# Splitting the last 256 queries of an attention kernel by token tile, with two one-tile FFNs side by side at the end, and limiting VectorE's share of the exps by its backlog

## The chip, the cores and the metric

One core of one Trainium2 chip. The metric is the device time of one execution in microseconds (us), lower is better; medians of several executions are quoted, and the 95% interval of the ratio where a verdict rests on it. The verdict limits are 2%.

Most of what follows hangs on one property of this program's executions: they come in two kinds, about 5 us apart, that differ in the mean clock that was granted to TensorE (PE). Where it matters I compare executions with a mean clock of 0.992 or more with each other ("high clock"), and those of 0.989 or less with each other ("low clock").

## The reference, cut to what matters

```python
def reference(A_x, A_wqkv, A_wo, B_x, B_w_gate, B_w_up, B_w_down, c, w_mod):
    # x: 1 x 2048 x 512 bf16; 32 heads of 16; FFN width 1792
    mod = (_silu(c) @ w_mod).reshape(...)            # sa, ca, ga, sb, cb, gb
    h = _layernorm(x) * (1 + ca) + sa
    x = x + ga * attention(h, A_wqkv, A_wo)          # softmax over 2048 keys, 32 heads
    h = _layernorm(x) * (1 + cb) + sb
    return x + gb * (_gelu(h @ w_gate) * (h @ w_up) @ w_down)
```

The softmax needs 32 x 2048 x 2048 exps. In blocks of 128 partitions x 512 columns that is 2048 blocks; the kernel calls one block a unit.

## The kernel before

The kernel is generated by a recorder with a small scheduler in it. While Python builds the program, the scheduler keeps a rough clock for each engine and decides in which order score matmuls (queries times keys), exps, PV matmuls (exps times values), "side work" (projections, FFNs of finished queries) and VectorE tasks are recorded. Each engine then runs its list in that order.

- ScalarE (ACT) takes three units at a time with one exp of 1536 columns. When VectorE (DVE) has room, it takes one of the three with a five-instruction polynomial, and ACT's exp is 1024 columns.
- Queries go in groups of 512, 512, 512, 256, 256. While the scores of one group run, the output projection, layernorm and FFN of the group before it run as side work through a single bank (`mi`) of PSUM, the memory that PE writes its results to.
- The last group has nothing behind it to hide under: `tail` does its projection, layernorm and FFN after the last exp.

```python
GROUPS = ((0, 512), (512, 512), (1024, 512), (1536, 256), (1792, 256))
...
RSTD = 13                     # 1/sqrt by 4 set-up steps and three Newton rounds of 3 tiny VectorE steps
...
# GELU of one chunk of the FFN, as side work
self.task([lambda: self.tt("dve", w, g, g, ALU.mult),
           lambda: self.ts("dve", w, w, GELU_C, 1.0, ALU.mult, ALU.add),
           lambda: self.tt("dve", w, w, g, ALU.mult),
           ("act", lambda: self.act(w, w, ACT.Tanh, scale=TANH_C0)),
           lambda: self.ts("dve", w, w, 1.0, None, ALU.add),
           lambda: self.tt("dve", w, w, g, ALU.mult)], ("gelu", gi, ci))
...
# may VectorE take the exp of unit g (15 to 18 units ahead)?
if (pos >= nsplit + 24 and len(active) < NACT and self.free["dve"] < t + 700
        and len(mem) == CH and slack > -100 and self.credit < 1024):
    g = pos + CH * LEAD
    ...
    if g >= nseq - 4 * LEAD or any(k not in self.have for k in self.keys(seq[g])):
        g = None
...
def tail(self, gi):           # the last 256 queries: two token tiles, one after the other
    ...
    for i in range(n):
        self.wo_mm(wob[i], gi, i, 7)
        self.wo_fin(wob[i], tiles[i])
        self.ln_stat(tiles[i])
    for f in self.ln2_steps(tiles):
        f()
    # ... transposes, then gate/up/down matmuls of both tiles together, 256 columns wide ...
    for i in range(n):
        self.down_fin(down[i], tiles[i])
```

`credit` counts how many matmul columns the side work is behind its plan (at most 4096): with 1024 or more, VectorE gets no exp.

The softmax here doesn't subtract the row's maximum and nothing guards it: scores larger than these inputs give would overflow.

## Time and profile before

| | before |
|---|---|
| device time, median of the first timed runs | 944.0 us (943.5 to 944.4) |
| device time of the profiled execution | 938.98 us (span 937.2) |
| first exp starts / last exp ends | 19.64 / 898.85 us |
| end after the last exp | 38.35 us |
| units that VectorE took | 149 of 2048 |
| time that ACT waited between exps | 1.1 us |

The profiled execution is 5 us faster than the timed ones.

The profile's page of the kernel before, its first lines (busy time and share of the span; then the busy share in 40 equal slices, in tenths):

```profile
span 937.2 us, 16746 instructions
PE 804.0 (86%) x6954; PEld 253.4 (27%) x6954; DVE 753.1 (80%) x1494; ACT 895.7 (96%) x756; POOL 7.2 (1%) x13
...
DVE  7735999999987999989997999988896772489643
ACT  6999999999999999999999999999999999999941
```

ACT is full from the first slices to the last two. VectorE is full only in between. PE's 86% contains dummy matmuls that the scheduler puts in when nothing else is there, so it is not a limit either.

The table by stage of the kernel before (stretch in us; its length; busy us and instruction counts of PE, weight loads, DVE, ACT and POOL; PE's granted clock; DMA share; GB/s):

```profile
core 0: us, PE busy (x) PEld busy (x) DVE busy (x) ACT busy (x) POOL busy (x), PEclk, DMA share, GB/s
50.00:100.00 50.00, 44.93 (x406) 16.49 (x404) 26.91 (x48) 49.85 (x44) 0.00 (x0) 1.00 0.24 84
750.00:800.00 50.00, 46.17 (x530) 15.33 (x525) 25.68 (x48) 50.00 (x39) 0.00 (x0) 1.00 0.06 16
900.00:937.00 37.00, 25.64 (x166) 16.62 (x166) 16.66 (x38) 6.49 (x10) 0.00 (x0) 0.90 0.02 8
```

VectorE has 23 of 50 us free near the start and 24 of 50 in 750 to 800 us while ACT is full. The last row is the end, where ACT is idle and PE's clock drops to 0.90.

The timeline of the kernel before, at the end (start, length, engine, line, operation, out<-in, shapes, count, and in brackets the idle time before it with what ended it):

```profile
878.74 20.10 ACT L304 ACTIVATE E<-ps_sc 128x1536 bf16<-128x1536 f32 x15
...
900.56 1.76 DVE L328 RECIPROCAL rb<-ps_mi 128x256 f32<-128x256 f32 x1 [0.79 <-PE ps_mi L291]
...
903.79 0.69 DVE L308 TENSOR_TENSOR xw<-ps_sc,ga 128x512 bf16<-128x512 f32 x1 [1.02 <-PE ps_sc L291]
...
910.27 0.74 DVE L316 TENSOR_SCALAR hreg<-xs,mv,rstd 128x512 bf16<-128x512 bf16 x2
910.74 1.25 PE L295 MATMUL ps_sc<-ident,hreg 128*128 128x128 bf16 x8 [6.77 <-DVE hreg L316]
...
912.23 5.70 PE L291 MATMUL ps_sc<-wreg,mreg 128*128 128x256 bf16 x32 [0.23 <-ACT wreg L304]
912.64 1.28 ACT L304 ACT_TABLE_LOAD   x1
...
934.60 0.42 DVE L308 TENSOR_TENSOR xs<-xs,xw 128x512 bf16<-128x512 bf16 x1
```

The last exp ends at 878.74 + 20.10 = 898.84. The softmax denominators, projection (903.79) and layernorm (910.27) of two tiles keep VectorE busy and PE waiting 6.77 us; then come 20 us of FFN on PE and two residual adds.

### The profile page before, as it was taken

What the parts mean: (1) busy time and instruction counts of PE and PEld (TensorE: products, weight loads), DVE (VectorE), ACT (ScalarE), POOL (GpSimd) and SP (SyncE); (2) the same over time, 40 slices, a digit from 0 to 9 for tenths busy, and PEclk for the clock granted to TensorE, in tenths of its full rate; (3) what the DMA queues carried; (4) which work ended last, traced back from release to release, by engine and by line L of the source; (5) the groups of instructions that cost most, each with busy time, mean ns of one, the idle gap of its engine ahead of it and who ended that gap; (6) DMA issues with size and microseconds to landing.
All of it is one profiled execution on the core that took longest, in us unless ns stands there. A gap on an engine that the chain in (4) does not pass through costs nothing.

```text
span 937.2 us, 16746 instructions
## 1 busy us (share of the span) xinstructions
PE 804.0 (86%) x6954; PEld 253.4 (27%) x6954; DVE 753.1 (80%) x1494; ACT 895.7 (96%) x756; POOL 7.2 (1%) x13
## 2 busy tenths in 40 slices
PE   7899888888888888888888888888898899888868
PEld 2333222222222222222222222222222233233325
DVE  7735999999987999989997999988896772489643
ACT  6999999999999999999999999999999999999941
POOL 3000000000000000000000000000000000000000
PEclk9999999999999999999999999999999999999999
DMA  8002700000000000000000000000000000000000
GB/s 292 1 1 66 226 6 13 13 13 14 13 13 13 2 13 13 13 19 20 24 13 2 13 12 13 13 14 21 11 25 14 13 8 20 24 13 8 19 12 12
DMA packets 31269, 25.05 MB, mean 27 GB/s; under 512 B 16061, under 2 KB 25978, under 8 KB 31194
## 3 DMA queue, kind: packets, MB, share of 16 engines
q1 hardware_dynamic: 28810, 22.42, 8.1%
q10 hardware_dynamic: 2384, 1.57, 0.6%
q8 instruction: 54, 0.88, 0.4%
q14 instruction: 21, 0.17, 0.1%
HBM read 21.36 MB, written 2.61 MB: 26 GB/s over the span
## 4 chain that ended last, share of the span: by engine, by line
ACT 90%; PE 4%; DVE 4%; DMA 1%; issue 0%; SPq 0%; DVEq 0%; ACTq 0%
ACT E L304 88%; PE ps_sc L291 3%; ACT wreg L304 3%; PE ps_mi L291 1%; DVE du L321 0%; PE ps_pv L291 0%; DVE st L344 0%; DVE xw L308 0%; DMA xs<-in_A_x_dram 0%; DVE dreg L316 0%; DVE nwt L308 0%; SPq L354 0%; DVE dt L316 0%; DVE sc_bf L316 0%; DVE kmo L316 0%
## 5 line engine op out<-in xcount | busy, mean ns | idle before, releaser
L304 ACT ACTIVATE E<-ps_sc 128x1536 bf16<-128x1536 f32 (+2 forms) x699 | 867.9, 1525 | 13.8 <-PE ps_sc L291 13.7
L291 PE MATMUL ps_pv<-E,vaug 128*17 128x512 bf16 (+1 forms) x2326 | 180.6, 337 | 1.5 <-ACT E L304 1.3
L291 PE MATMUL ps_sc<-qT,kme 32*128 32x512 bf16 (+1 forms) x1280 | 152.0, 340 | 27.7 <-ACT E L304 22.8
L291 PE MATMUL ps_sc<-qT,kmo 32*128 32x512 bf16 (+1 forms) x1280 | 153.2, 340 | 25.9 <-ACT E L304 21.3
L316 DVE TENSOR_SCALAR dt<-ps_sc 128x512 int32<-128x512 f32 x149 | 102.8, 690 | 38.2 <-PE ps_sc L291 35.2
L291 PE MATMUL ps_sc<-xs,ident 128*128 128x512 bf16 x271 | 90.3, 386 | 46.1 <-ACT E L304 43.5
L291 PE MATMUL ps_mi<-wreg,mreg 128*128 128x512 bf16 (+1 forms) x448 | 119.8, 357 | 8.7 <-DVE hreg L308 4.4
L321 DVE SCALAR_TENSOR_TENSOR ED<-du,dt 128x512 int16<-128x512 f32 x149 | 101.5, 683 | 1.3
L321 DVE SCALAR_TENSOR_TENSOR du<-du,dt 128x512 f32<-128x512 f32 x149 | 100.6, 681 | 0.2
L321 DVE SCALAR_TENSOR_TENSOR du<-dt 128x512 f32<-128x512 uint16 x149 | 100.1, 682 | 0.1
L291 PEld LDWEIGHTS ps_sc<-qT,kme 32*128 32x128 bf16 x1280 | 39.0, 91 | 143.3 <-ACT E L304 107.6
L291 PEld LDWEIGHTS ps_sc<-qT,kmo 32*128 32x128 bf16 x1280 | 39.4, 91 | 139.2 <-ACT E L304 101.0
L291 PEld LDWEIGHTS ps_pv<-E,vaug 128*17 128x17 bf16 x2326 | 45.9, 87 | 99.2 <-issue 89.5
L291 PE MATMUL ps_mi<-dreg,hreg 128*128 128x512 bf16 x210 | 67.2, 385 | 1.6 <-DVE xw L308 1.0
L316 DVE TENSOR_SCALAR dt<-dt 128x512 f32<-128x512 int32 x149 | 61.5, 416 | 0.6
L291 PE MATMUL ps_pv<-ED,vaug 128*17 128x512 bf16 (+1 forms) x170 | 56.3, 356 | 0.0
L291 PEld LDWEIGHTS ps_mi<-wreg,mreg 128*128 128x128 bf16 x448 | 35.2, 97 | 68.9 <-issue 32.0
L308 DVE TENSOR_TENSOR wreg<-wreg 128x1024 bf16<-128x1024 bf16 (+1 forms) x84 | 51.9, 618 | 0.8
L325 DVE CAST wreg<-ps_mi 128x512 bf16<-128x512 f32 x49 | 33.7, 688 | 19.2 <-PE ps_mi L291 18.5
L291 PEld LDWEIGHTS ps_sc<-xs,ident 128*128 128x128 bf16 x271 | 19.6, 97 | 99.4 <-ACT E L304 97.1
L291 PE MATMUL ps_mi<-hreg,wreg 128*128 128x512 bf16 x120 | 39.8, 386 | 1.5 <-DVE vaug L325 0.7
L308 DVE TENSOR_TENSOR hreg<-ps_mi,wreg 128x512 bf16<-128x512 f32 x49 | 33.7, 688 | 8.7 <-PE ps_mi L291 8.0
(109 smaller groups left out, 514.7 us busy)
## 6 DMA issues: line engine op xcount, KB each, us to landing
rb<-scr_rec SPq DMA_DIRECT2D x96, 64.0 KB, 2.0
mreg<-in_w_mod_dram SPq DMA_DIRECT2D x1, 2048.0 KB, 13.1
out_dram<-xs SPq DMA_DIRECT2D x16, 128.0 KB, 1.7
rb<-scr_rec SPq DMA_DIRECT2D x60, 32.0 KB, 1.8
mreg<-in_B_w_gate_dram SPq DMA_DIRECT2D x1, 1792.0 KB, 7.2
mreg<-in_B_w_up_dram SPq DMA_DIRECT2D x1, 1792.0 KB, 12.0
dreg<-in_B_w_down_dram SPq DMA_DIRECT2D x1, 1792.0 KB, 19.9
wreg<-in_A_wqkv_dram SPq DMA_DIRECT2D x3, 384.0 KB, 10.5
```

Of the source, the lines that this page charges most:

```text
L291: return self.rec("pe", lambda e: e.matmul(out, lhsT, rhs, start=start, stop=stop, tile_position=tp), [lhsT, rhs], [out], cost=(n, int(rhs ...
L304: return self.rec("act", lambda e: e.activation(out, in_, func, scale=scale, **kw), rd, wr, cost=self.cost("act", out, [in_], "act"))
L308: return self.rec(eng, lambda e: e.tensor_tensor(out, a, b, op), [a, b], [out], cost=self.cost(eng, out, [a, b], "tt"))
L316: return self.rec(eng, lambda e: e.tensor_scalar(out, a, s1, s2, **kw), rd, [out], cost=self.cost(eng, out, [a], "ts"))
L321: return self.rec("dve", lambda e: e.scalar_tensor_tensor(out, a, s, b, op0=op0, op1=op1), rd, [out], cost=self.cost("dve", out, [a, b], " ...
L325: return self.rec(eng, lambda e: e.tensor_copy(out, in_), [in_], [out], cost=self.cost(eng, out, [in_], "ts"))
```

## The change

Its intent: the last 256 queries stay one 256-wide unit for head quads 0 to 5 (a quad is four heads), but quads 6 and 7 are scored first for token tile 14 alone, then for tile 15 alone. Tile 14 is thus finished 32 units (about 14 us) before the last exp; its projection and layernorm run under the remaining exps, and at the end its FFN runs next to tile 15's softmax, projection and layernorm. Around this, VectorE's load is changed: exps may start at unit 16 instead of 152, but only with fewer than 8 runnable steps waiting and fewer than three unconsumed exps; GELU loses one pass; the Newton iteration for 1/sqrt loses one round.

```diff
-GROUPS = ((0, 512), (512, 512), (1024, 512), (1536, 256), (1792, 256))
+SETS = ((0, 512), (512, 512), (1024, 512), (1536, 256), (1792, 128), (1920, 128))
+QS = 6
+BACK = 8
+DPOS = 16
...
-    RSTD = 13
+    RSTD = 10
...
-                               ("act", lambda: self.act(w, w, ACT.Tanh, scale=TANH_C0)),
-                               lambda: self.ts("dve", w, w, 1.0, None, ALU.add),
-                               lambda: self.tt("dve", w, w, g, ALU.mult)], ("gelu", gi, ci))
+                               ("act", lambda: self.act(w, w, ACT.Tanh, scale=TANH_C0))], ("gelu", gi, ci))
...
-                self.tt("dve", self.prodT[...], mi[...], w[...], ALU.mult)
+                self.stt(w[...], w[...], 1.0, mi[:, 0:W * k], ALU.add, ALU.mult)
+                if b0 + kpb >= m:
+                    self.tt("dve", self.prodT[...], w[...], g[...], ALU.mult)
...
+        due = (ends[1] + 30, ends[2] + 30, ends[3] + 30, n - 32, n)
...
+        units = [((k,), qd) + SETS[k] for k in range(4) for qd in range(8)]
+        units += [((4, 5), qd, SETS[4][0], 2 * P) for qd in range(QS)]
+        units += [((k,), qd) + SETS[k] for k in (4, 5) for qd in range(QS, 8)]
...
-                if (pos >= nsplit + 24 and len(active) < NACT and self.free["dve"] < t + 700
+                if (pos >= DPOS and len(active) < NACT and sum(v >= 4 * rp for v in vec) < 3
+                        and self.backlog() < BACK and self.free["dve"] < t + 700
                         and len(mem) == CH and slack > -100 and self.credit < 1024):
...
-    def tail(self, gi):
+    def tail(self, ka, kb):
+        self.act(self.tcol[:, 0:1], self.tcol[:, 0:1], ACT.Gelu_apprx_tanh)
+        gens = [self.tail_end(kb), self.tail_ffn(ka, self.pv[:, :], range(0, 4), 0)]
+        # ... at each step the generator whose next matmul is ready first goes on ...
```

`due` says by which unit each FFN of the side work has to be done; the third-last FFN (tiles 12 and 13) must now end 32 units before the end instead of 9.

## The prediction

> **What bounds the kernel now.** ScalarE's exp. The page gives ACT 895.7 of 937.2 us busy (96%), and the chain of waits is ACT 90%. In the table by stage ACT is full (50.0 of 50) from 20 us to 898.9 us; then 38.3 us follow with ACT nearly idle. By shape, ACT runs 515 exps of 1536 columns and 177 of 1024, issued 1.34 and 0.92 us apart (timeline), so one 512-column unit costs ACT 0.43 us. VectorE takes 149 of the 2048 units, five instructions, about 3.2 us each. PE is filled up with 309 dummy matmuls (ps<-xs,ident); it does not bound. So only two things count: fewer units on ACT, and a shorter end.
>
> **The end (main gain).** In the timeline, after the last exp: 11.4 us of copy, reciprocal, output projection, layernorm (two tiles one after the other, 13 rstd steps 0.2 us apart) before the first transpose at 910.7; PE waits 6.8 us there and its clock falls (0.90 in this stretch); table load 1.28 us; FFN of two tiles to 932.4; two serial residual steps and a store to 937.2. The change finishes tile 14's attention 32 units (about 14 us) earlier, so its projection and layernorm run under the last exps and its FFN fills the time in which tile 15 goes through reciprocal, projection and layernorm. Matmuls of 128 columns cost no more per column: 16 took 1.07 us (57 ns each), 256-column ones 109 ns. So each one-tile FFN is about 112x57 ns + 14x213 ns = 9.4 us of PE. Estimate: tile 15's chain 9-10 us (half widths, 10 steps), then 9.4 us FFN, then 3.5-5 us: about 25 us instead of 38.3. Gain 13, less about 1 us for denser PE work and VectorE work near the end.
>
> **VectorE.** (a) Exps may start at unit 16 instead of 152. VectorE is busy 26.9 of 50 us in 50-100 us and never takes an exp before 88 us; I expect about 7 more there, 3 us of ACT. (b) GELU loses one 0.42 us pass per 1024-column chunk net (a 0.42 and a 0.68 us pass go, a 0.68 us one comes; the multiply from PSUM stays 0.69 us[...]). [...] About 9 us of VectorE, 2-3 exps, 1 us. (c) Three rstd steps fewer: 0.6 us on the chain before the first exp; elsewhere small. (d) The backlog limits delay exps but do not lower VectorE's capacity; in 100-700 us it is 93% busy anyway. In 700-850 us only 7 exps run, though VectorE has 50 us free; I think side-work credit holds them back, and the change leaves that as it is. I expect 155-165 exps in all.
>
> **Sum.** 13 - 1 + 3 + 1 + 0.6 = about 16 us: 928 us, range 921 to 937. Faster by over 2% means below 925: 0.33; within 2%: 0.63; slower: 0.04.
>
> **What would show it.** From last exp to end 23-28 us, with ps_sc<-wreg,mreg matmuls starting within about 2 us of the last exp, and PE clock near 1.0 there. ED count 155-165 with several before 88 us. ACT still 100% busy from 19 us to about 900.
>
> **What would make it wrong.** Tile 14's layernorm not ready at the last exp (its side work queues behind the third-last FFN, which must now end 23 units earlier): the end stays above 30 us. ACT waiting for PE in the last 28 us, where scores and PV come in twice as many 128-column matmuls. The limit of three unconsumed VectorE exps cutting them in 150-700 us: each lost costs 0.43 us. Or the better VectorE order letting many more exps in at 700-850 us: then 920.

(13 - 1 + 3 + 1 + 0.6 is 16.6, put as about 16, and 944 - 16 is 928. The 1 us taken off for denser work near the end was an allowance of mine with no trace behind it.)

## The result, and the profile after

The first timed runs: 930.5 us after (929.99 to 936.03) against 944.0 before (943.51 to 944.41), ratio 0.987 with a 95% interval of 0.983 to 0.991, and inside the predicted range.

The page of the kernel after:

```profile
span 928.6 us, 17403 instructions
PE 801.0 (86%) x7308; PEld 258.5 (28%) x7308; DVE 743.1 (80%) x1448; ACT 897.8 (97%) x760; POOL 7.2 (1%) x13
...
DVE  6737899988987999998886999999888664378745
ACT  6999999999999999999999999999999999999992
```

The table by stage of the kernel after:

```profile
50.00:100.00 50.00, 45.08 (x400) 15.93 (x399) 30.65 (x54) 50.00 (x45) 0.00 (x0) 1.00 0.32 107
750.00:800.00 50.00, 45.89 (x520) 15.01 (x519) 23.10 (x42) 50.00 (x40) 0.00 (x0) 1.00 0.08 20
900.00:928.60 28.60, 23.05 (x324) 17.41 (x318) 14.61 (x37) 9.33 (x16) 0.00 (x0) 0.98 0.03 11
```

The holes of VectorE are still there: 19 us free in 50 to 100 (23 before), 27 in 750 to 800 (24 before). The end is shorter, its PE is busy 23.05 of 28.6 us, and its clock stays at 0.98.

The timeline of the kernel after, at the end:

```profile
882.85 19.15 ACT L309 ACTIVATE E<-ps_sc 128x1536 bf16<-128x1536 f32 x14
...
895.32 0.69 DVE L313 TENSOR_TENSOR xw<-ps_mi,ga 128x512 bf16<-128x512 f32 x1 [2.69 <-PE ps_mi L296]
900.40 0.31 DVE L321 TENSOR_SCALAR hreg<-xs,mv,rstd 128x512 bf16<-128x512 bf16 x1
902.01 1.28 ACT L309 ACT_TABLE_LOAD   x1
904.68 0.83 PE L296 MATMUL ps_sc<-wreg,mreg 128*128 128x128 bf16 x12
906.13 3.07 PE L296 MATMUL ps_sc<-wreg,mreg 128*128 128x128 bf16 x52
911.38 0.41 DVE L321 TENSOR_SCALAR du<-xs,mv,rstd 128x512 bf16<-128x512 bf16 x1
912.77 3.22 PE L296 MATMUL ps_sc<-wreg,mreg 128*128 128x128 bf16 x48
...
925.92 0.42 DVE L313 TENSOR_TENSOR xs<-xs,xw 128x512 bf16<-128x512 bf16 x1
```

Tile 14's projection is added at 895.32 and its layernorm is written at 900.40 (`hreg`), before the last exp ends at 902.00. Its FFN starts at 904.68. Tile 15's layernorm is written at 911.38 (`du`): in the 7 us between, PE works on tile 14 where it used to wait.

So the end went from 38.35 to 26.60 us, near the predicted 25. But the spans differ by only 8.6 us (937.2 to 928.6), and 11.75 of gain at the end plus 1.67 at the start minus 8.6 leaves 4.8 us that the exp phase lost. VectorE took 147 units, not the 155 to 165 that I expected.

### The profile page after: what moved, and what is told of

It reads as the page before. It is cut to its first block, busy times and chain, and to the rows that moved or that the text cites. A ratio compares the mean times of both kernels' runs of the same rounds, so it can differ in the third digit from the quotient of the medians. Undisturbed runs are those within 1.5% of the kernel's fastest.

```text
span 928.6 us, 17403 instructions
## 1 busy us (share of the span) xinstructions
PE 801.0 (86%) x7308; PEld 258.5 (28%) x7308; DVE 743.1 (80%) x1448; ACT 897.8 (97%) x760; POOL 7.2 (1%) x13
## 4 chain that ended last, share of the span: by engine, by line
ACT 91%; PE 4%; DVE 2%; DMA 1%; issue 0%; SPq 0%; DVEq 0%; ACTq 0%
ACT E L309 88%; PE ps_sc L296 3%; ACT wreg L309 3%; PE ps_mi L296 1%; DMA scr_rec<-rden 1%; PE ps_pv L296 1%; DMA xs<-in_A_x_dram 0%; DVE xw L313 0%; DMA rb<-scr_rec 0%; DVE sc_bf L321 0%; PE ps_mi L300 0%; DVE st L349 0%; DVE dreg L321 0%; ACT xw L309 0%; ACT L309 0%
## 5 line engine op out<-in xcount | busy, mean ns | idle before, releaser
L296 PE MATMUL ps_pv<-E,vaug 128*17 128x512 bf16 (+2 forms) x2452 | 179.8, 330 | 1.8 <-ACT E L309 1.2
L296 PE MATMUL ps_sc<-qT,kme 32*128 32x512 bf16 (+2 forms) x1344 | 155.6, 333 | 28.4 <-ACT E L309 22.7
L296 PE MATMUL ps_sc<-qT,kmo 32*128 32x512 bf16 (+2 forms) x1344 | 153.3, 332 | 30.2 <-ACT E L309 26.0
L296 PEld LDWEIGHTS ps_sc<-qT,kme 32*128 32x128 bf16 x1344 | 41.3, 91 | 147.3 <-ACT E L309 106.7
L296 PE MATMUL ps_pv<-ED,vaug 128*17 128x512 bf16 (+2 forms) x172 | 55.0, 351 | 0.0
L330 DVE CAST wreg<-ps_mi 128x512 bf16<-128x512 f32 x49 | 33.8, 689 | 24.7 <-PE ps_mi L296 24.6
L326 DVE SCALAR_TENSOR_TENSOR wreg<-wreg,ps_mi 128x512 bf16<-128x512 bf16 x49 | 33.6, 685 | 11.1 <-PE ps_mi L296 8.0
L296 PE MATMUL ps_mi<-wo,onorm 128*128 128x512 bf16 x120 | 36.5, 384 | 0.7 <-DVE xw L313 0.5
## 6 DMA issues: line engine op xcount, KB each, us to landing
wreg<-in_A_wqkv_dram SPq DMA_DIRECT2D x3, 384.0 KB, 10.5
```

Source lines behind the costliest of these rows:

```text
L296: return self.rec("pe", lambda e: e.matmul(out, lhsT, rhs, start=start, stop=stop, tile_position=tp), [lhsT, rhs], [out], cost=(n, int(rhs ...
L326: return self.rec("dve", lambda e: e.scalar_tensor_tensor(out, a, s, b, op0=op0, op1=op1), rd, [out], cost=self.cost("dve", out, [a, b], " ...
L330: return self.rec(eng, lambda e: e.tensor_copy(out, in_), [in_], [out], cost=self.cost(eng, out, [in_], "ts"))
```

## The experiments

Twelve kernels ran, all correct. Each has six timed runs (`e4_credit_due` five), and each set that was sent together has eleven runs of the kernel before on the same chip.

### The account that all of them are read with

From each trace I took the start of the first exp, the end of the last one, the waits of ACT between them, and the number of units that VectorE took. The waits are those of the exps for scores, as `--waits` sums them. Each row is one profiled execution, of whichever kind it happened to be.

| kernel | mean clock | first exp | last exp ends | VectorE units | ACT waits | end | span |
|---|---|---|---|---|---|---|---|
| before | 0.994 | 19.64 | 898.85 | 149 | 1.1 | 38.35 | 937.2 |
| `c0_before_again` | 0.994 | 18.55 | 898.25 | 149 | 1.4 | 39.55 | 937.8 |
| after | 0.994 | 17.97 | 902.00 | 147 | 4.7 | 26.60 | 928.6 |
| `c1_after_again` | 0.999 | 17.98 | 898.50 | 147 | 1.9 | 26.60 | 925.1 |
| `e1_vector_only` | 0.984 | 17.98 | 903.13 | 150 | 6.6 | 38.27 | 941.4 |
| `e2_split_only` | 0.994 | 18.55 | 905.38 | 148 | 6.9 | 33.42 | 938.8 |
| `e5_serial` | 0.989 | 18.86 | 902.22 | 147 | 4.1 | 32.98 | 935.2 |
| `e8_qs0` | 0.989 | 19.59 | 908.66 | 139 | 5.2 | 30.04 | 938.7 |
| `e3_credit` | 0.987 | 17.97 | 896.73 | 161 | 4.5 | 33.77 | 930.5 |
| `e4_credit_due` | 0.998 | 17.95 | 894.02 | 160 | 2.1 | 26.68 | 920.7 |
| `e3b_credit_all` | 0.993 | 19.05 | 889.07 | 172 | 1.5 | 45.63 | 934.7 |
| `e6_no_limits` | 0.998 | 17.97 | 897.33 | 152 | 2.3 | 26.67 | 924.0 |
| `f1_before_warm` | 0.989 | 18.41 | 901.86 | 149 | 3.7 | 38.24 | 940.1 |
| `f2_credit_no_limits` | 0.990 | 18.83 | 896.51 | 161 | 4.0 | 26.69 | 923.2 |

Two regularities carry the rest. First, (last exp - first exp) + 0.427 us x VectorE units - ACT waits is 941.4 to 943.4 us in all fourteen rows. This is little more than the sum of ACT's work, so it shows where time went and not why; but with it the exp phase can be read from two numbers, the units taken off ACT and ACT's waits. (In the trace of before, exps of 1536 columns are 1.331 us apart from start to start and those of 1024 columns 0.904, medians; the difference is 0.427.) Second, in all fourteen traces it is 23.9 to 25.5 us from the first FFN matmul after the last exp (`ps_sc<-wreg,mreg`) to the end. So the length of the end follows how long after the last exp that matmul starts: 2.7 us in the five rows with an end of 26.6 to 26.7, 5.6 in `e8_qs0`, 7.9 to 8.8 in `e5_serial`, `e3_credit` and `e2_split_only`, 12.8 to 15.0 with the old ending, 20.3 in `e3b_credit_all`. The clock goes along with it: by the clock records the nine longer ends hold 3.41 to 10.24 us at 0.50 (a last stretch that the end of the program cuts left out), the five short ones none.

### Controls: the two kernels again

No edit.

> Control: the kernel before, unchanged. Its profiled run took 938.98 us, its four timed runs 943.5 to 944.4, while the kernel after agrees with its profile (930.35 against 929.99 to 930.64) but for one run of 936.03 at clock 0.984. Theory: every run of either kernel falls in one of two variants, about 5 us apart, by where a stretch of half clock falls early in the run; the profile of before is of the short one. Then the runs of before here show two clusters, near 939 and near 944, and the long ones have a lower mean clock (about 0.984 against 0.994). Rival: the profiled execution of before is an oddity and all timed runs stay at 944 with clock 0.994.

> Control: the kernel after, unchanged. Theory of two variants: runs near 930 (clock 0.994) and near 936 (clock 0.984), about 5.7 us apart; like against like the change is worth 8 to 9 us (938.98 against 930.35), not 13.5. Rival: all near 930, and the change is worth 13.5 us.

Measured: `c0_before_again` 941.2 us median (939.3 to 945.2), `c1_after_again` 929.4 (926.9 to 936.1). All 50 runs of the kernel before for which the clock is listed (these six and those beside four sets of experiments) fall into two heaps with nothing between:

| | high clock: runs, mean (range) | low clock: runs, mean (range) |
|---|---|---|
| before, 50 runs | 18, 939.2 (938.5 to 940.6) | 32, 944.2 (942.7 to 945.6) |
| after, 10 runs | 7, 929.3 (926.9 to 930.6) | 3, 935.1 (933.2 to 936.1) |

The theory of two kinds is right. Like against like the change is worth 9.9 us (high) or 9.1 us (low). The 13.5 us of the first medians are a mixture: by their times, all first timed runs of before were of the slow kind, and three of four of after were of the fast one. Whether the change itself makes the high kind commoner (7 of 10 runs against 18 of 50) is not shown, ten runs are too few; if it does, comparing like with like leaves a part of its gain out.

The table by stage of the kernel after shows what a low-clock stretch looks like:

```profile
20.00:25.00 5.00, 5.00 (x33) 1.78 (x31) 4.01 (x12) 4.12 (x4) 0.00 (x0) 0.50 0.35 134
25.00:30.00 5.00, 5.00 (x27) 1.48 (x26) 3.37 (x9) 3.61 (x5) 0.00 (x0) 0.55 0.00 0
```

And the same program in the control, `c1_after_again`:

```profile
20.00:25.00 5.00, 4.18 (x44) 1.61 (x42) 4.86 (x15) 4.99 (x6) 0.00 (x0) 1.00 0.37 143
25.00:30.00 5.00, 4.58 (x38) 1.60 (x38) 4.86 (x16) 5.00 (x5) 0.00 (x0) 1.00 0.00 0
```

At half clock PE is 100% busy and still too slow: ACT is busy 7.73 of 10 us instead of 9.99. That is where 2.3 of the 4.8 us lost in the exp phase of the first profile of after went. The half-clock stretch there lasts 10.2 us; in the clock records of all fourteen profiles every such stretch, but for the last one of each that the end of the program cuts, is 3.41, 6.83 or 10.24 us long, in steps of 3.41 us. Executions of one program that catch more or fewer such stretches would fit the heaps; that the heaps are just this is my guess and not shown. Between the two controls, which both run at full clock from 18 us to the last exp (as the table by stage gives it), the exp phase lost only 0.82 us: 0.85 for two units fewer on VectorE, 0.5 of waits, and -0.5 unexplained. The rest is -0.57 at the start and -12.95 at the end, and the sum is the -12.7 us of the spans.

### VectorE's parts alone, and the split alone

`e1_vector_only` is the kernel before with the new VectorE parts and the old ending; `e2_split_only` is the kernel after with them undone.

```diff
 # e1_vector_only, on the kernel before
-    RSTD = 13
+    RSTD = 10
 # ... GELU, layernorm order of the first stage, DPOS = 16, BACK = 8 and both limits as in the change ...

 # e2_split_only, on the kernel after
-    RSTD = 10
+    RSTD = 13
 # ... GELU and layernorm order as before, exps from unit 152 on, no limits ...
```

> The kernel before with all VectorE parts of the change (10 rstd steps, shorter GELU, exps from unit 16, the limits, layernorm order) and the old ending of 256 queries together. Recorded program: 150 VectorE exps against 149. Theory A (the VectorE parts save only the 0.6 us of rstd before the first exp, since the exp count hardly moves): at clock 0.992 or more 938 to 939.5 us against 939.3 of before; the end after the last exp 38 less 0.6. Rival B (the VectorE parts carry a good part of the gain): 934 or less.

> The kernel after with the VectorE parts undone (13 rstd steps, the old GELU, exps only from unit 152, no limits): the split and the two-FFN ending alone. Recorded program: 148 exps; the layernorm of tile 14 is not recorded before the last exp. Theory A (the whole gain is the ending): as the kernel after, 929 to 931 at clock 0.992 or more. Rival B (the ending only pays when tile 14's layernorm is done before the last exp, and the VectorE parts and limits are what gets it done in time): the end after the last exp is 30 to 33 us instead of 26.6, and the time 934 to 939.

Measured: `e1_vector_only` 942.1 us, ratio to before 0.999 (0.997 to 1.002). All its six runs were of low clock (mean 942.2, before 944.2 to its side at low clock), so the number that I had written for high clock has nothing to be compared with; like with like it gains about 2 us. `e2_split_only` 944.2 us, ratio 1.001 (0.998 to 1.004); its two high-clock runs took 939.7 and 940.6, as before.

Each half alone is worth nothing or next to nothing, and both together 9 to 10 us. Rival B is the nearer one for the split, though both of its numbers were missed a little (33.4 us at the end against 30 to 33, 940.1 at high clock against 934 to 939). In the account its end is 33.4 us instead of 26.6, and ACT waits 6.9 us instead of 1.1 to 1.9. The timeline of `e2_split_only` shows both, first one of its waits, then tile 14 at the end:

```profile
583.75 0.69 DVE L330 CAST wreg<-ps_mi 128x512 bf16<-128x512 f32 x1 [0.20 <-PE ps_mi L296]
584.36 0.68 DVE L326 SCALAR_TENSOR_TENSOR ED<-du,dt 128x512 int16<-128x512 f32 x1
584.50 0.39 PE L296 MATMUL ps_mi<-wreg,mreg 128*128 128x512 bf16 x1 [0.79 <-DVE wreg L330]
585.10 0.38 PE L296 MATMUL ps_pv<-ED,vaug 128*17 128x512 bf16 x1
585.42 0.39 PE L296 MATMUL ps_sc<-qT,kme 32*128 32x512 bf16 x3
585.86 1.45 ACT L309 ACTIVATE E<-ps_sc 128x1536 bf16<-128x1536 f32 x1 [2.04 <-PE ps_sc L296]
...
904.85 0.69 DVE L313 TENSOR_TENSOR xw<-ps_mi,ga 128x512 bf16<-128x512 f32 x1 [3.71 <-PE ps_mi L296]
907.77 0.10 DVE L321 TENSOR_SCALAR nwx<-mv 128x1 f32<-128x1 f32 x1
```

At 583.75 VectorE, with exps interleaved, empties the PSUM bank late; PE stands at 584.50 for that bank, then takes PV of a VectorE exp (`ED`, written only just before), and the scores that ACT needs stand behind them in PE's list until 585.42. ACT waits 2.04 us, at full clock; another wait at full clock, of 1.51 us, is at 713 us. Of the 6.9 us, 2.2 lie in or just after two half-clock stretches (from 22.86 and from 616.78 us, 3.41 us each). At the end, tile 14's projection is added at 904.85, 0.5 us before the last exp ends (6.7 us before it in the kernel after), and its layernorm has not begun. Against `c0_before_again`, 6.1 us were gained at the end and 7.1 lost in the exp phase. The two have the same mean clock, but not in the same places: all half-clock stretches of `c0_before_again` come after its last exp.

Which of the VectorE parts it takes to get tile 14 done in time I did not test one by one on the chip. That the two limits are not needed for it is shown below by `e6_no_limits`.

### Does the overlap of the two FFNs matter?

`e5_serial`: tile 14's FFN waits for tile 15's layernorm; nothing else changes.

```diff
 def tail_ffn(self, k, down, banks, e0):
-        yield from self.until(("ln2", k))
+        yield from self.until(("ln2", len(SETS) - 1))
```

> The kernel after, but tile 14's FFN at the end waits for the layernorm of tile 15, so nothing fills the wait. Same program up to the last exp. Theory (PE work of tile 14's FFN under tile 15's chain is what shortens the end): in the trace of after 0.83+3.07+1.03+1.95 us, about 7 us of that FFN runs before tile 15's layernorm is done, so the end grows by 5 to 7 us, to 32 to 33 us. Rival (the gain is the earlier projection and layernorm of tile 14, not the overlap): the end grows by less than 2 us.

Measured: 937.7 us median, one high-clock run at 935.7. The end is 32.98 us, 6.4 longer than in after. The timeline of `e5_serial` shows PE idle again where it was filled:

```profile
905.15 0.39 PE L300 MATMUL ps_sc<-ident,hreg 128*128 128x128 bf16 x4
909.68 0.61 PE L300 MATMUL ps_sc<-ident,du 128*128 128x128 bf16 x4 [4.14 <-DVE du L321]
910.08 8.03 PE L296 MATMUL ps_sc<-wreg,mreg 128*128 128x128 bf16 x96
```

So of the 11.7 us by which the end got shorter, the overlap is worth 6.4. A part of that is clock and not idle time alone: PE's clock is 0.50 from 908.50 to 915.33 us in `e5_serial`, and full in the end of after until 927.17. The rest I put down to narrower work, without a run that takes it apart: half-width reciprocals (0.95 us in after, 1.76 in before), one tile's adds instead of two, three steps fewer. The last layernorm is written 7.0 us after the last exp in `e5_serial` and 11.8 us after it in before, which is 4.8 of the remaining 5.3 us.

### How wide should the split be?

`e8_qs0` splits all eight head quads.

```diff
-QS = 6
+QS = 0
```

> The split widened from the last two to all eight head quads, so tile 14 is finished 128 units before the end instead of 32. Recorded program: 139 VectorE exps instead of 147, and four times as many 128-column score and PV matmuls. Theory (ScalarE is the limit, and each exp lost by VectorE costs 0.43 us): last exp 3.4 us later, plus waits of ScalarE for PE; end after it 26 to 28 us as in after; 932.5 to 936 at clock 0.992 or more. Rival (denser small matmuls make PE the limit there): ScalarE waits over 5 us in the last 60 us and the time is over 938.

Measured: 938.5 us median; high clock 935.8 (three runs), inside the 932.5 to 936 of the theory. VectorE took 139 units, which is 3.4 of the 5.0 us by which its exp phase is longer than in the first profile of after. Of the waits of ACT, 5.2 us, 3.5 lie at 111 to 115 us and 183 us in the trace and 0.7 at 829 to 834, none in the last 60, so the rival is out: the denser small matmuls do not make PE the limit. The end was 30.0 rather than the 26 to 28 that I expected. Its timeline, after the last exp at 908.66, says why:

```profile
910.76 0.41 DVE L321 TENSOR_SCALAR hreg<-xs,mv,rstd 128x512 bf16<-128x512 bf16 x1
914.30 0.42 PE L296 MATMUL ps_sc<-wreg,mreg 128*128 128x128 bf16 x2
```

Though tile 14's attention was finished 96 units earlier than in after, its layernorm is written 2.1 us after the last exp (1.6 us before it in after), and its first FFN matmul starts 5.6 us after it; the clock is 0.50 from 911.59 to 915.00 us. Two quads are the better of the two widths that ran: the wider split lost 8 VectorE exps and 3.4 us at the end.

### What holds VectorE's exps back?

VectorE has free time, but credit must be below 1024. Counted while the program of the kernel after is generated, credit was too high in 40 of the 67 times that VectorE was asked in the scheduler's first 100 us, and in 69 of 69 from 700 to 800 us. ("Asked" is every time that the scheduler comes to the test from unit 16 on. Often another condition fails too: credit alone stood in the way in 15 of the 67 and 36 of the 69.) Three kernels lift the limit: below unit 1400 (`e3_credit`), the same with an earlier due date for the FFN of tiles 12 and 13 (`e4_credit_due`), and everywhere (`e3b_credit_all`).

```diff
 # all three: keep the record of finished K and Q honest (see below)
         self.work = self.plan(ends, nsplit)
+        self.have = {x for x in self.have if x[0] == "v"} | {("k", 0, 0), ("q", 0, 0)}
 # e3_credit and e4_credit_due
-                        ... and self.credit < 1024):
+                        ... and self.credit < (4096 if pos < 1400 else 1024)):
 # e3b_credit_all
+                        ... and self.credit < 4096):
 # e4_credit_due
-        due = (ends[1] + 30, ends[2] + 30, ends[3] + 30, n - 32, n)
+        due = (ends[1] + 30, ends[2] + 30, ends[3] + 30, n - 40, n)
```

The first line mends a flaw that the kernel has before and after: planning runs each side task once dry, and the dry run marks every K, Q and V tile as finished. The test whether a unit's K is ready can then never fail. As long as VectorE seldom takes early units this does no harm; with the credit limit lifted, a score matmul read K before it was written. With the line alone, the program of the kernel after is unchanged on PE, VectorE and ACT.

> The kernel after with the side-work credit limit on VectorE exps lifted from 1024 to 4096 for units below 1400 (and the scheduler's record of finished K and Q kept honest, which alone leaves the program of after unchanged). Recorded program: 161 exps instead of 147; but tile 14's layernorm is not recorded before the last exp. Theory (credit, not VectorE time, held the early exps back): about 8 exps before 100 us, the last exp about 5 to 6 us earlier than in after, the end 5 to 7 us longer (32 us), time 928 to 931. Rival (VectorE cannot do more exps without delaying PE's side work until ScalarE waits): ScalarE waits over 5 us more and the last exp is not earlier.

> As the run with the credit limit lifted below unit 1400, and the third-last FFN due 8 units earlier (40 before the end). Recorded program: 160 exps, and tile 14's layernorm is recorded before the last exp. Theory (both levers add: 13 exps more at 0.43 us, and the short end): last exp 4.5 to 6 us earlier than in after, end 26 to 27 us, time 923 to 925.5 at clock 0.992 or more. Against the run without the earlier due date this isolates the readiness of tile 14: 5 to 7 us. Rival: the end is the same in both (readiness does not matter on the chip), difference under 2 us.

> The credit limit at 4096 over the whole run. Recorded program: 172 exps instead of 147 and side work of the last sets left over at the end. Theory: last exp about 9 to 10 us earlier than in after, but the end grows by 15 to 18 us to about 43 us because the third-last FFN is unfinished: 935 to 938. So the credit limit is what keeps the idle VectorE of 700 to 850 us unused, and lifting it there only moves the work to the end. Rival (VectorE is not free there): last exp under 5 us earlier.

Measured:

| | median | high clock | VectorE units | end |
|---|---|---|---|---|
| `e3_credit` | 930.6 | 928.8 (3 runs) | 161 | 33.77 |
| `e4_credit_due` | 922.4 | 922.6 (all 5 runs) | 160 | 26.68 |
| `e3b_credit_all` | 936.7 | 936.3 (2 runs) | 172 | 45.63 |

The theory of credit holds. `e4_credit_due` took 10 units within the first 100 us (before 2, after 4), and its last exp ended 4.5 us earlier than that of `c1_after_again`; its time came out just under the 923 to 925.5 that I had expected. In the exps of VectorE by stage of `e3b_credit_all` (busy time of the instruction that writes `ED`), there are now exps where the kernels before and after have none in 750 to 800 us:

```profile
700.00:750.00 50.00, 3.44 (x5) 1.00 0.05 12
750.00:800.00 50.00, 4.71 (x8) 1.00 0.05 11
800.00:850.00 50.00, 6.15 (x9) 1.00 0.09 24
```

But that is not free time to be had for nothing: its last exp ends 9.4 us earlier and its end is 19.0 us longer (I had put it at 15 to 18), because the FFN of tiles 12 and 13 is left over. The timeline of `e3b_credit_all`, after its last exp at 889.07:

```profile
891.92 3.20 PE L296 MATMUL ps_mi<-dreg,hreg 128*128 128x512 bf16 x14 [0.56 <-DVE xw L313]
...
909.40 2.88 PE L296 MATMUL ps_sc<-wreg,mreg 128*128 128x128 bf16 x25 [0.79 <-DVE nwt L313]
```

Fourteen down-projection matmuls of an older tile (`dreg,hreg`) still run at 891.92, and tile 14's FFN starts only at 909.40.

`e3_credit` and `e4_credit_due` differ by one unit on VectorE and by the 8 units of the due date. Their timelines say what the 7.1 us between their ends are. First `e3_credit`, last exp at 896.73:

```profile
896.19 0.69 DVE L313 TENSOR_TENSOR xw<-ps_mi,ga 128x512 bf16<-128x512 f32 x1 [3.57 <-remote]
903.26 0.38 DVE L321 TENSOR_SCALAR hreg<-xs,mv,rstd 128x512 bf16<-128x512 bf16 x1
905.09 3.22 PE L296 MATMUL ps_sc<-wreg,mreg 128*128 128x128 bf16 x28 [0.79 <-DVE rstd L330]
```

Then `e4_credit_due`, last exp at 894.02:

```profile
887.35 0.69 DVE L313 TENSOR_TENSOR xw<-ps_mi,ga 128x512 bf16<-128x512 f32 x1 [2.90 <-PE ps_mi L296]
892.43 0.31 DVE L321 TENSOR_SCALAR hreg<-xs,mv,rstd 128x512 bf16<-128x512 bf16 x1
896.70 0.83 PE L296 MATMUL ps_sc<-wreg,mreg 128*128 128x128 bf16 x12
```

Tile 14's layernorm (`hreg`) comes 6.5 us after the last exp in the one and 1.6 us before it in the other, and its first FFN matmul 8.4 against 2.7 us after it. That decides between an end of 33 to 34 and of 26.7 us, here as in `e2_split_only` (layernorm 7.0, first FFN matmul 8.8 us after the last exp); `e8_qs0` lies between them.

`e4_credit_due` is the best version: 922.4 us, ratio to before 0.979 with an interval of 0.976 to 0.982, and 6.7 us below the high-clock mean of after. At nearly the same clock the lead is smaller: 922.4 (0.998) against 926.9 (0.999), and 923.7 against 928.6 at 0.996. Part of its lead over the medians of others is that none of its five runs was of low clock; I can't say whether that is its doing or luck.

### Are the two limits needed?

`e6_no_limits` takes both limits out of the kernel after; `f2_credit_no_limits` adds the lifted credit below unit 1400.

```diff
-                if (pos >= DPOS and len(active) < NACT and sum(v >= 4 * rp for v in vec) < 3
+                if (pos >= DPOS and len(active) < NACT
-BACK = 8
+BACK = 99
```

> The kernel after without the two new limits (backlog of 8 steps, three unconsumed VectorE exps), with the honest record of K and Q. Recorded program: 152 exps instead of 147, tile 14's layernorm still recorded before the last exp. Theory (the limits cost 5 exps, 2 us, and are not what makes the end short): 926 to 928 at clock 0.992 or more. Rival (without limits VectorE runs late on the chip and PE and ScalarE wait): ScalarE waits 3 us more and time is 929 or more.

> The credit limit lifted below unit 1400 as in the two runs before it, without the two new limits and with the third-last FFN due as in after. Recorded program: 161 exps, tile 14's layernorm recorded before the last exp. By the account of the other runs (last exp minus first exp plus 0.427 us per VectorE exp minus ScalarE's waits is 942 us): last exp at 18 + 942 - 68.7 + 2 = 893 us, end 26.7, span 920, time 921 to 923, as the best run so far (922.4) or 1 us better. Rival (without limits the waits grow once the exps are denser): waits above 5 us, 925 or more.

Measured: `e6_no_limits` 928.2 us median, 927.4 in its five runs of 0.992 or more, as the theory had it: five VectorE units more than in after, the short end, waits of 2.3 us. In this combination the limits cost 1 to 2 us: 1.9 by the high-clock means, 1.2 by the runs of highest clock (925.7 at 0.998, after 926.9 at 0.999). `f2_credit_no_limits` 925.0 us median (921.2 to 929.6), ratio to before 0.982 (0.978 to 0.986, "unclear" by the 2% rule), above the expected 921 to 923; its profile shows waits of 4.0 us, more than I had put in (2), and its runs spread over all clocks from 0.982 to 0.996, one of them at 921.2. Against `e4_credit_due` that is inconclusive.

### Where do the low-clock runs come from?

`f1_before_warm` puts 16 more dummy matmuls into the first 20 us of the kernel before, to keep PE busy.

```diff
-        self.warm_up(10)
+        self.warm_up(20)
...
+        self.warm_up(2)
         self.proj_k(0, 0, self.scp[:, 4, :], "both")
         self.proj_q(0, 0, self.scp[:, 5, :], act)
+        self.warm_up(4)
```

> The kernel before with 16 more dummy matmuls in the prologue (10 while PE waits for the activated condition vector, 2 before the first projection, 4 after it); the order of the rest is the same. Theory (the 944 us variant of before comes from PE losing its full clock in the thin first 20 us and early on, as the 0.5 clock stretches at 18 to 30 us in two profiles suggest): the low-clock runs vanish or get rare, the runs gather at 938.5 to 940, clock 0.992 or more; median 4 us lower than before. Rival (the low-clock stretches lie elsewhere, in the stream, or come by chance whatever the prologue does): both variants stay, median 942 to 945.

Measured: 941.5 us median (938.1 to 943.0), clocks 0.987 to 0.996, both kinds as before; in its own profile the clock is 0.50 from 21.05 to 31.29 us. The theory that a thin prologue is to blame, and can be mended this way, fell. What starts the low-clock stretches stays open, but the kept traces narrow it. Cut from 6 to 890 us into the 3.41 us steps that the stretches keep to, they hold 25 steps at full clock in which PE is busy for less than 2.1 us; half clock follows 17 of these 25, and 10 of the other 3542. One of the 17 is in after: PE is busy 2.06 us from 15.82 to 19.23 us, and 10.24 us at 0.50 follow. So 17 of the 27 stretches begin after a step in which PE has little to do, anywhere in the program. That is a correlation; no run tested it. A busy PE did not rule a stretch out: in `e1_vector_only` the clock fell to 0.59 in 84 to 86 us, after PE had been busy 5.50 of the 6 us before. Nor did it end one at once: in after PE was busy without a gap from 19.45 us on, by the (modelled) times of the matmuls, and the clock stayed at 0.50 until 29.47 us.

## Why the prediction was right or wrong

The time, 930.5 us, lies in the predicted range of 921 to 937, and the class "within 2%" was the likeliest. The gain that I had worked out was 16 us; like with like it is 9 to 10. Point by point:

- **The end: right.** "About 25 us instead of 38.3. Gain 13, less about 1 us": 26.6 us, 11.75 less than in the profile that I read. The first FFN matmul came 2.7 us after the last exp, not 2: ACT does the first modulation, and the table load for the GELU comes before it: it began at 902.01, 0.01 us after the last exp ended, and took 1.28 us, and the next activation began at 903.31. PE's clock was 0.98 there. `e5_serial` shows that 6.4 us of it are the overlap, and `e2_split_only` and `e3_credit` that 7 us hang on tile 14's layernorm being done at the last exp, the first of the things that I had named as able to make the prediction wrong. It was done in this program, so it did not bite; in the split alone it was not, and with the 7.1 us lost in the exp phase that is why the split alone gained nothing.
- **The first exp: right.** "0.6 us" for three 1/sqrt steps fewer; 18.55 to 17.98 between the controls, 0.57. (The 1.67 us between the first two profiles hold 1.1 us more: that of before has a half-clock stretch from 14.96 to 18.37 us.)
- **VectorE's load: right, its use: wrong. This is the term that was mis-sized.** I expected 9 us of VectorE time from GELU; in the page's totals `e1_vector_only` has 746.0 us of VectorE time against 753.2 of `c0_before_again`, 7.2 less with one exp more. The new multiply and the old one both read the PSUM bank `mi`, and the new one takes as long as the old (685 ns in after, 688 in before, for 512 columns). But I turned that time, and the free time before 88 us, into exps: "155-165 exps in all", worth 3 + 1 us. The program has 147, two fewer than before, worth -0.9 us. That is a miss of about 5 us. I had seen that "side-work credit holds them back" at 700 to 850 us, and did not ask whether the same test also holds them back in the first 100 us. It does: with it lifted there and up to unit 1400, VectorE takes 160, 10 of them in the first 100 us where after has 4.
- **The limits: wrong.** "The backlog limits delay exps but do not lower VectorE's capacity": without them it is 152 units instead of 147, and the high-clock mean is 1.9 us lower (927.4 to 929.3, at somewhat higher clocks). (VectorE's busy share in 100 to 700 us of before is 90%, not the 93% that I wrote.)
- **The sum: the parts do not add.** I treated ending, exps and VectorE load as separate terms. `e1_vector_only` and `e2_split_only` show that they are not: 2 us at most and nothing alone, 9 to 10 together.
- **What I did not see: two kinds of execution.** My base of 944 was of the slow kind and the profile of the fast one. That the sum of 928 came within 2.5 us of the measured 930.5 is luck: 16 us, too large a gain, taken from a base of the slow kind, meets a median of the fast kind.

## What to carry to other kernels

When a tail is hidden by starting part of it earlier, what decides is whether that part's last dependence is done when the critical engine stops; check that one instant in the trace. The loss grows with the lateness: a first FFN matmul 2.7, 5.6, 8.4 and 20.3 us after the last exp went with ends of 26.6, 30.0, 33.8 and 45.6 us. An idle engine is an offer only if what keeps it idle is known: here a scheduler's rule about another engine's backlog, and lifting it shortened the exp phase by 0.34 to 0.42 us per exp (4.45 us for 13 in `e4_credit_due`, 10.5 for 25 in `e3b_credit_all`, against `c1_after_again`), up to the point where it pushed the backlog into the tail. And before a gain of 1% is explained, list the clock of every run beside its time.
